# Top-k attention with a squared-ReLU feed-forward layer: a third search round over 264 columns, and v loaded in pieces of 1 KB

## The chip, the core and the metric

The kernel runs on one core of a Trainium2 chip. The core has five engines with queues of their own: TensorE (PE in the profile; PEld is its weight load), VectorE (DVE), ScalarE (ACT), GpSimd (POOL) and SyncE (SP), which here only issues transfers. Sixteen DMA engines move data between the memory of the chip (DRAM) and the core, and inside the core. The metric is device time in microseconds (us); less is better.

## The reference

There are 8 batches with 8 heads of 576 positions and 64 values each. For every query row the 576 scores are computed, the 32 largest are kept, and a softmax over those weighs the rows of v. The result, 4608 tokens of 512 values, goes through a feed-forward layer with 2048 hidden values.

```python
scores = scale * np.matmul(q, k.transpose(0, 1, 3, 2))
kth = np.partition(scores, -top_k, axis=-1)[..., -top_k:-top_k + 1]   # top_k = 32
scores = np.where(scores >= kth, scores, -1000000000.0)
attn = softmax(scores)
x = np.matmul(attn, v)                # then to [4608, 512]
out = np.square(np.maximum(x @ w_in, 0.0)) @ w_out
```

Inputs and outputs are float32.

## The kernel before

**Steps.** The work on the scores is cut into 144 steps (`steps`, L224 to L241). A step holds 128 query rows of two heads, side by side in the tile's middle axis `x`, so nearly everything is done for x = 0 and x = 1. The order of the instructions on each engine is the order in which the program issues them (`pin`). The main loop (L688) works on step u and, in the same turn, on parts of steps u+1 (scores) and u-1 to u-4 (weights, products, placing).

**Scores.** `scores` (L251) multiplies in two halves of 288 columns into the PSUM tiles `sc_a` and `sc_b` (L263), and ScalarE copies both into `s` (L266).

**Sorting into halves.** Before the search VectorE and GpSimd arrange the 576 scores of a row in a tile `cat`. `pairs_of` (L282, L283) takes the larger of columns n and n + 288; `quads_of` (L291, L292) compares the larger ones again, 144 apart: the larger go to columns 0 to 143 of `cat`, the smaller to 144 to 287. `both` (L307) and `lesser` (L316) put the lesser of each first pair, as sum minus larger, into columns 288 to 575 on GpSimd; `copy_far` (L298) copies what GpSimd needs out of PSUM on ScalarE. In the first 20 steps (`EARLY`) a quarter of this is done by VectorE (L285). Large scores thus gather on the left.

**The search.** `topk` finds the 32nd largest score in four rounds. Each round takes the eight largest of some columns with one MAX8 for each x (L342); the first three also overwrite them with a very negative number, with MATCH_REPLACE8 and the value load that goes before it (L346). The rounds read growing parts of `cat` (`part`, L333): 104 columns, then 120, then the left half of 288, then all 576. The fourth round's eighth value is the threshold. That is right only if the first three rounds took nothing smaller than it; L351 to L353 note for each row whether a round's eighth value lies below the fourth's, and if any row shows that, the program runs `general` (L788) at the end, which does the whole task in a plain way.

**Order on VectorE in a step.** `quads_of(u)`, round 1, the reciprocal of step u-4 (L436), rounds 2 and 3, `pairs_of(u+1)`, round 4.

**After the search.** `drop` (L378) marks on GpSimd what lies under the threshold, and a transfer from GpSimd's queue adds the marks to `s` (L382); ScalarE takes exponentials (L386); a transposing transfer on SP's queue turns them (L395); TensorE multiplies with v (L422), with a column of ones for the sum; ScalarE scales and stores (L452, L459). The feed-forward products (L533, L556) are fed in between in small pieces (`dense`, `piece`).

**Loads.** `load_pair` queues the loads of a pair of heads: for q, k and v one load of 512 rows for each head and one or two loads of the last 64 rows. `fetch` issues a few of these in each step on SP's queue; `load_first` issues those of the first pair on the queues of SP and ScalarE. All three tiles were laid out alike, as [128, 5, 2, 64]: partition p holds rows 4p to 4p+3, for each row the 64 values of head 0 and then those of head 1, and last the remaining rows. TensorE transposes q and k from there (`main`, `first_step`); `values` (L204) casts v to bf16 into `va` on ScalarE, with L206 for the 512 rows and L209 for the rest.

Of the kernel before, what the change touches and what calls it, by code (L numbers as in the profile page):

```python
# [13 lines left out]
f32 = mybir.dt.float32  # L14
# [4 lines left out]
AF = mybir.ActivationFunctionType  # L19
# [4 lines left out]
def kernel(  # L24
# [9 lines left out]
    nc = tc.nc  # L34
    B, H, S, D = q.shape
# [7 lines left out]
    HALF, QUAR = S // 2, S // 4  # L43

    def pin(ins):
        tc.keep_in_program_order(ins)
        return ins
# [3 lines left out]
    ld = fast.enter_context(tc.tile_pool(name="ld", bufs=2))  # L51
# [40 lines left out]
    raw, prep = {}, {}  # L92

    fetches = []

    def load_pair(i):
        b, pr = pairs[i]
        raw[i] = [None] * 3

        def whole_rows(z, name, two, a):  # L100
            def go():
                if a == 0:
                    raw[i][z] = ld.tile([128, 5, 2, 64], f32, name=name)
                pin(nc.sync.dma_start(out=raw[i][z][:, 0:4, a, :], in_=two[a, 0:512].rearrange("(p c) d -> p c d", c=4)))
            return go

        def rest_rows(z, two, at):
            def go():
                pin(nc.sync.dma_start(out=raw[i][z][at:at + 64, 4], in_=two[:, 512:576].rearrange("h p d -> p h d")))
            return go  # L110

        for z, (name, src) in enumerate((("q_raw", q), ("k_raw", k), ("v_raw", v))):
            two = src[b, 2 * pr:2 * pr + 2]
            for a in range(2):
                fetches.append((i, whole_rows(z, name, two, a)))
            fetches.append((i, rest_rows(z, two, 0)))
            if z == 2:
                fetches.append((i, rest_rows(z, two, 64)))
# [5 lines left out]


    def load_first():
        raw[0] = [ld.tile([128, 5, 2, 64], f32, name=name) for name in ("q_raw", "k_raw", "v_raw")]
        at = [z[0, 0:2] for z in (q, k, v)]

        def rows(queue, z, a):  # L130
            pin(queue.dma_start(out=raw[0][z][:, 0:4, a, :], in_=at[z][a, 0:512].rearrange("(p c) d -> p c d", c=4)))

        def last(queue, z, to=0):
            pin(queue.dma_start(out=raw[0][z][to:to + 64, 4], in_=at[z][:, 512:576].rearrange("h p d -> p h d")))

        for z in (1, 0):
            rows(nc.sync, z, 0)
            rows(nc.scalar, z, 1)
        last(nc.sync, 1)
        last(nc.scalar, 0)  # L140
        rows(nc.sync, 2, 0)
        rows(nc.sync, 2, 1)
        last(nc.sync, 2)
        last(nc.sync, 2, 64)

    def prep_units(i):
        q_raw, k_raw, v_raw = raw[i]
        qkT = heads.tile([128, 512 + 640], f32, name="qkT")
        qT, kT = qkT[:, 0:512], qkT[:, 512:1152]
        k_rest = kT.rearrange("p (n d) -> p n d", d=64)[:, 0:10:9]  # L150
        bd, va = qbd[i % 5], vau[i % 6]
        prep[i] = (qT, kT, bd, va)

        def twice(t):
            return t.rearrange("p (o d) -> p o d", o=1).broadcast_to([128, 2, 64])

        def main(which, src):
            def go():
                tp = ps_one.tile([128, 512], f32, name="gen", bufs=2)
                for c in range(4):  # L160
                    pin(nc.tensor.transpose(tp[:, c * 128:(c + 1) * 128], src[:, c], id_f[:, :]))
                pin(nc.scalar.activation((qT, kT[:, 64:576])[which], tp[:, :], AF.Copy, scale=(scale, 1.0)[which]))
            return go


        def first_step():
            for j, bank in ((0, "gen"), (1, "gen"), (2, "dn_ps"), (3, "sc_a")):
                if bank == "sc_a":
                    tp = ps_sc.tile([128, 2, 512], f32, name=bank)[:, 0, :]
                else:  # L170
                    tp = ps_one.tile([128, 512], f32, name=bank, bufs=2 if bank == "gen" else None)
                if j < 2:
                    for c in range(2):
                        pin(nc.tensor.transpose(tp[:, c * 128:(c + 1) * 128], k_raw[:, 2 * j + c], id_f[:, :]))
                    to, got = kT[:, 64 + j * 256:64 + (j + 1) * 256], tp[:, 0:256]
                elif j == 2:
                    pin(nc.tensor.transpose(tp[:, 0:128], q_raw[:, 0], id_f[:, :]))
                    to, got = qT[:, 0:128], tp[:, 0:128]
                else:
                    pin(nc.tensor.transpose(tp[:, 0:64], k_raw[0:64, 4], id_f[0:64, 0:64]))  # L180
                    to, got = k_rest, twice(tp[:, 0:64])
                if j % 2:
                    pin(nc.vector.tensor_copy(to, got))
                else:
                    pin(nc.scalar.activation(to, got, AF.Copy, scale=scale if j == 2 else 1.0))

        def first_q():
            tp = ps_one.tile([128, 512], f32, name="gen", bufs=2)
            for c in range(1, 4):
                pin(nc.tensor.transpose(tp[:, c * 128:(c + 1) * 128], q_raw[:, c], id_f[:, :]))  # L190
            pin(nc.scalar.activation(qT[:, 128:512], tp[:, 128:512], AF.Copy, scale=scale))

        def rest(both=(0, 1)):
            tp = ps_one.tile([128, 512], f32, name="gen", bufs=2)
            for which in both:
                src = (q_raw, k_raw)[which]
                pin(nc.tensor.transpose(tp[:, which * 64:(which + 1) * 64], src[0:64, 4], id_f[0:64, 0:64]))
            if 0 in both:
                pin(nc.scalar.activation(bd[0:64, 0:64], tp[0:64, 0:64], AF.Copy, scale=scale))
                pin(nc.scalar.activation(bd[64:128, 64:128], tp[64:128, 0:64], AF.Copy, scale=scale))  # L200
            if 1 in both:
                pin(nc.scalar.activation(k_rest, twice(tp[:, 64:128]), AF.Copy))

        def values():  # L204
            assert i < 6 or av_left[i - 6] == 0
            pin(nc.scalar.activation(va[:, 0:4, :, 0:64], v_raw[:, 0:4], AF.Copy))  # L206
            for x in range(2):
                half = slice(64 * x, 64 * x + 64)
                pin(nc.scalar.activation(va[half, 4 + x, :, 0:64], v_raw[half, 4], AF.Copy))  # L209

        if i == 0:
            return [first_step, first_q, values, lambda: rest((0,))]
        return [main(0, q_raw), main(1, k_raw), rest, values]
# [11 lines left out]
    for b in range(B):  # L225
        p0 = 4 * b
        if b == B - 1:
            at = [((0, 0), (1, 0), (2, 0), (0, 1), (3, 0), (1, 1), (2, 1), (3, 1)), [(j, 2) for j in range(4)], [(j, 3) for j in range(4)]]
            at = [[whole(p0 + j)[c] for j, c in some] for some in at]
# [94 lines left out]
    def topk(u, rounds=(0, 1, 2, 3)):  # L324
        d = st[u]
        g = u % GROUP
        if g == 0 and 0 in rounds:
            held_m["m"] = small.tile([128, GROUP, 2, 4, 8], f32, name="m", bufs=2)
        held = held_m["m"]
        m = d["m"] = [held[:, g, :, r] for r in range(4)]  # L330
        d["ends"] = held[:, g].rearrange("p x r j -> p x (r j)")[:, :, 0:32:31]
        cat = d["cat"]
        def part(r, x):  # L333
            if r == 0:
                return cat[:, x, 0:QUAR].rearrange("p (g n) -> p g n", n=18)[:, :, 0:13]
            if r == 1:
                return cat[:, x, 0:QUAR].rearrange("p (g n) -> p g n", n=6)[:, :, 1:6]
            return cat[:, x, 0:(HALF, S)[r - 2]]

        for r in rounds:  # L340
            for x in range(2):
                pin(nc.vector.max(out=m[r][:, x, :], in_=part(r, x)))  # L342
            if r == 3:
                break
            for x in range(2):
                pin(nc.vector.match_replace(out=part(r, x), in_to_replace=m[r][:, x, :], in_values=part(r, x), imm_value=NEG))  # L346
        if g == GROUP - 1 and 3 in rounds:
            f0 = 2 * (u + 1 - GROUP)
            each = held[:, :, :, :, 7].rearrange("p g x r -> p (g x) r")
            at = flags[:, f0:f0 + 2 * GROUP]  # L350
            pin(nc.gpsimd.tensor_tensor(at[:, :, 0:3], each[:, :, 3:4].broadcast_to([128, 2 * GROUP, 3]), each[:, :, 0:3], op=ALU.subtract))  # L351
            pin(nc.gpsimd.tensor_mul(at[:, :, 3], each[:, :, 3], each[:, :, 3]))
            pin(nc.gpsimd.tensor_scalar(at[:, :, 3], at[:, :, 3], scalar1=-1.0, scalar2=TINY * TINY, op0=ALU.mult, op1=ALU.add))  # L353
# [557 lines left out]
```

## Time and profile before

| | |
|---|---|
| median of three runs | 940.04 us (935.3, 940.04, 949.31) |
| profiled execution | 938.25 us |
| its span, first to last instruction | 936.5 us |
| mean granted TensorE clock | 0.933 |
| instructions | 20941 |
| transfers | 329978 packets, 166.29 MB |

The time of an execution is longer than the span by what lies before the first and after the last instruction. In the profile's groups, a line such as "L342 DVE MAX8 m<-cat 128x8 f32<-128x288 f32 x288 | 120.4, 472 | 0.0" reads: line of the program, engine, operation, output and input tile, their shapes, how often; then busy microseconds in total and mean nanoseconds of one; then how long the engine stood idle just before such instructions, and what ended the wait. The chain of work that ended last is followed back from the last instruction, at each step to what released it; "issue" on it is time in which the engine waited for nothing that the profile shows. Busy times of one engine overlap in the records, so the sum of its groups is more than its busy time.

### The profile page before, as it was taken

What the parts mean: (1) busy time and instruction counts of PE and PEld (TensorE: products, weight loads), DVE (VectorE), ACT (ScalarE), POOL (GpSimd) and SP (SyncE); (2) the same over time, 40 slices, a digit from 0 to 9 for tenths busy, and PEclk for the clock granted to TensorE, in tenths of its full rate; (3) what the DMA queues carried; (4) which work ended last, traced back from release to release, by engine and by line L of the source; (5) the groups of instructions that cost most, each with busy time, mean ns of one, the idle gap of its engine ahead of it and who ended that gap; (6) DMA issues with size and microseconds to landing.
All of it is one profiled execution on the core that took longest, in us unless ns stands there. A gap on an engine that the chain in (4) does not pass through costs nothing.

```text
span 936.5 us, 20941 instructions
## 1 busy us (share of the span) xinstructions
PE 678.4 (72%) x6176; PEld 429.6 (46%) x6176; DVE 898.1 (96%) x3637; ACT 784.2 (84%) x1776; POOL 778.8 (83%) x803
## 2 busy tenths in 40 slices
PE   6777667777776778767786777767766687777777
PEld 3333344444444445444454444444444455554554
DVE  5999999999999999999999999999989999999993
ACT  4777888889888988889887998888978998997984
POOL 7888889888888888888888889888878887898780
PEclk9988999899999998999989999999979998999899
DMA  5568866899998999889999998989999999787761
GB/s 140 132 159 166 174 137 125 173 200 198 205 209 172 201 203 199 187 191 198 195 202 182 187 206 195 207 182 191 176 191 207 188 206 195 160 174 164 148 138 39
DMA packets 329978, 166.29 MB, mean 178 GB/s; under 512 B 306561, under 2 KB 306561, under 8 KB 329857
## 3 DMA queue, kind: packets, MB, share of 16 engines
q1 hardware_dynamic: 311088, 92.62, 52.2%
q0 software_dynamic: 17568, 71.97, 33.9%
q8 instruction: 52, 0.85, 0.4%
q14 instruction: 70, 0.57, 0.2%
q10 hardware_dynamic: 1200, 0.30, 0.1%
HBM read 37.75 MB, written 9.44 MB: 50 GB/s over the span
## 4 chain that ended last, share of the span: by engine, by line
DVE 70%; issue 10%; PE 8%; ACT 6%; DMA 5%; POOL 1%; SPq 0%; ACTq 0%; POOLq 0%
DVE m L342 29%; DVE cat L346 18%; DVE sc_b L282 6%; DVE cat L292 5%; DVE cat L291 5%; DVE most L283 5%; PE dn_ps L556 2%; PE sc_b L263 2%; PE gen L533 1%; PE sc_a L263 1%; DMA wT<-w_two_a 1%; DMA wT<-w_two_c 1%; ACT s L266 1%; DVE rsum L436 1%; DMA v_raw<-in_v_dram 1%
## 5 line engine op out<-in xcount | busy, mean ns | idle before, releaser
L342 DVE MAX8 m<-cat 128x8 f32<-128x104 f32 (+3 forms) x1152 | 461.2, 455 | 0.0
L346 DVE MATCH_REPLACE8 cat<-m,cat 128x104 f32<-128x104 f32 (+2 forms) x864 | 281.1, 346 | 0.0
L307 POOL TENSOR_TENSOR cat<-s 128x576 int32<-128x576 int32 (+1 forms) x144 | 230.2, 1598 | 3.8 <-ACT s L266 3.8
L316 POOL TENSOR_TENSOR cat<-cat,most 128x576 int32<-128x576 int32 (+1 forms) x144 | 190.3, 1322 | 26.4 <-ACT most L298 15.6
L263 PE MATMUL sc_b<-qkT 64*128 64x288 f32 x512 | 109.2, 502 | 127.3 <-DVE cat L292 125.5
L533 PEld LDWEIGHTS <-w_in 128*128 128x128 bf16 x2304 | 149.6, 103 | 49.5 <-issue 28.5
L556 PE MATMUL dn_ps<-w_out,h 128*128 128x512 bf16 x576 | 165.0, 417 | 1.5 <-ACT wide L561 1.5
L533 PE MATMUL gen<-xT,w_in 128*128 128x128 bf16 x2016 | 140.7, 226 | 12.7 <-ACT rl L538 6.0
L266 ACT ACTIVATE s<-sc_b 128x576 f32<-128x576 f32 x144 | 93.4, 648 | 66.2 <-PE sc_b L263 59.8
L378 POOL TENSOR_SCALAR gone_a<-s,neg 128x576 uint8<-128x576 f32 x143 | 107.1, 749 | 29.5 <-ACT neg L361 20.2
L263 PE MATMUL sc_a<-qkT 64*128 64x288 f32 x512 | 99.7, 464 | 40.9 <-DVE most L283 30.0
L378 POOL TENSOR_SCALAR gone_b<-s,neg 128x576 uint8<-128x576 f32 x142 | 106.4, 749 | 27.3 <-ACT neg L361 17.7
L263 PEld LDWEIGHTS sc_b<-qkT 64*128 64x128 f32 x512 | 47.4, 206 | 177.2 <-issue 102.0
L266 ACT ACTIVATE s<-sc_a 128x576 f32<-128x576 f32 x144 | 91.5, 635 | 20.2 <-PE sc_a L263 19.7
L538 ACT ACTIVATE rl<-gen 128x512 f32<-128x512 f32 x142 | 85.1, 600 | 5.5 <-PE gen L533 4.4
L544 ACT ACTIVATE h<-rl 128x512 bf16<-128x512 f32 x136 | 85.8, 631 | 4.3
L346 DVE MATCH_VALUE_LOAD cat<-m,cat 128x8 f32 x864 | 89.1, 103 | 0.0
L422 PEld LDWEIGHTS <-wT 128*128 128x128 bf16 (+1 forms) x1600 | 59.0, 101 | 63.7 <-DMA wT<-w_two_c 24.2
L556 PEld LDWEIGHTS <-h 128*128 128x128 bf16 x576 | 54.4, 104 | 66.5 <-issue 31.0
L282 DVE TENSOR_TENSOR sc_b<-sc_a,s 128x288 f32<-128x288 f32 x144 | 69.6, 484 | 6.1 <-ACT s L266 6.0
L386 ACT ACTIVATE w_two_a<-s,neg 128x576 bf16<-128x576 f32 x96 | 69.4, 779 | 5.0 <-DMA s<-gone_b 3.0
L291 DVE TENSOR_TENSOR cat<-sc_b,most 128x288 f32<-128x288 f32 x144 | 67.3, 467 | 5.2 <-ACT most L298 5.0
(165 smaller groups left out, 1201.4 us busy)
## 6 DMA issues: line engine op xcount, KB each, us to landing
s<-gone_a POOLq DMA_DIRECT2D x61, 576.0 KB, 4.9
s<-gone_b POOLq DMA_DIRECT2D x61, 576.0 KB, 4.7
v_raw<-in_v_dram SPq DMA_DIRECT2D x64, 128.0 KB, 3.2
out_dram<-wide SPq DMA_DIRECT2D x32, 256.0 KB, 3.6
k_raw<-in_k_dram SPq DMA_DIRECT2D x63, 128.0 KB, 3.3
q_raw<-in_q_dram SPq DMA_DIRECT2D x63, 128.0 KB, 3.2
wide<-in_moe_w_in_dram SPq DMA_DIRECT2D x8, 512.0 KB, 4.7
wide<-in_moe_w_out_dram SPq DMA_DIRECT2D x8, 512.0 KB, 4.1
```

What stands on the lines that cost most here:

```text
L263: pin(nc.tensor.matmul(out=ps[j][:, x, 0:HALF], lhsT=lhsT, rhs=rhs, start=True, stop=True))
L266: pin(nc.scalar.activation(s[:, :, j * HALF:(j + 1) * HALF], ps[j][:, :, 0:HALF], AF.Copy))
L282: pin(tt(far, one[:, :, QUAR:HALF], two[:, :, QUAR:HALF], op=ALU.max))
L291: pin(tt(cat[:, :, 0:QUAR], far, near, op=ALU.max))
L307: pin(tt(less, s[:, :, 0:wide].bitcast(i32), s[:, :, HALF:HALF + wide].bitcast(i32), op=ALU.add))
L316: pin(tt(less, less, d["most"][:, 0:n_h, :, :].bitcast(i32).rearrange("p h x n -> p x h n"), op=ALU.subtract))
L342: pin(nc.vector.max(out=m[r][:, x, :], in_=part(r, x)))
L346: pin(nc.vector.match_replace(out=part(r, x), in_to_replace=m[r][:, x, :], in_values=part(r, x), imm_value=NEG))
L378: pin(nc.gpsimd.tensor_scalar(byte[:, x, :, 1], s[:, x, :], scalar1=d["neg"][:, x, 1:2], scalar2=-HUGE, op0=ALU.add, op1=ALU.mult))
L533: pin(nc.tensor.matmul(out=hp[:, n * n_rows:(n + 1) * n_rows], lhsT=w_in[:, kh, (f0 + n) * 128:(f0 + n + 1) * 128], rhs=xt(kh), start=(kh ...
L544: pin(nc.scalar.activation(h2, flat, AF.Square))
L556: pin(nc.tensor.matmul(out=op[:, :], lhsT=held["h2"][:, f, c * 128:(c + 1) * 128], rhs=w_out[:, f, :], start=(f == 0), stop=(f == NF - 1)))
```

## The change

Two things are edited. First, the third round reads columns 0 to 263 of `cat` in place of 0 to 287; the fourth still reads all 576. Second, the tile `v_raw` is laid out head by head: partition p holds the four rows of head 0 one after the other, then those of head 1, then the remaining rows as before. A load of 512 rows of one head thus writes 256 values in a row (1 KB) in each partition, where it wrote four runs of 64 values (256 bytes). The cast in `values` reads the new layout and writes `va` as before. The loads keep their number, queue and order.

```diff
+    def by_head(t):
+        return t.rearrange("p (a d) -> p a d", a=2)
...
-                    raw[i][z] = ld.tile([128, 5, 2, 64], f32, name=name)
+                    raw[i][z] = ld.tile([128, 640] if z == 2 else [128, 5, 2, 64], f32, name=name)
+                if z == 2:
+                    pin(nc.sync.dma_start(out=raw[i][z][:, a * 256:(a + 1) * 256], in_=two[a, 0:512].rearrange("(p c) d -> p (c d)", c=4)))
+                    return
                 pin(nc.sync.dma_start(out=raw[i][z][:, 0:4, a, :], in_=two[a, 0:512].rearrange("(p c) d -> p c d", c=4)))
...
-                pin(nc.sync.dma_start(out=raw[i][z][at:at + 64, 4], in_=two[:, 512:576].rearrange("h p d -> p h d")))
+                t = raw[i][z]
+                to = by_head(t[at:at + 64, 512:640]) if z == 2 else t[at:at + 64, 4]
+                pin(nc.sync.dma_start(out=to, in_=two[:, 512:576].rearrange("h p d -> p h d")))
...
-            pin(nc.scalar.activation(va[:, 0:4, :, 0:64], v_raw[:, 0:4], AF.Copy))
+            pin(nc.scalar.activation(va[:, 0:4, :, 0:64], v_raw[:, 0:512].rearrange("p (a c d) -> p c a d", a=2, c=4), AF.Copy))
             for x in range(2):
                 half = slice(64 * x, 64 * x + 64)
-                pin(nc.scalar.activation(va[half, 4 + x, :, 0:64], v_raw[half, 4], AF.Copy))
+                pin(nc.scalar.activation(va[half, 4 + x, :, 0:64], by_head(v_raw[half, 512:640]), AF.Copy))
...
-            return cat[:, x, 0:(HALF, S)[r - 2]]
+            return cat[:, x, 0:(HALF - 24, S)[r - 2]]
```

`load_first` is changed in the same way for the first pair.

More of the change, by code (lines that the diff above doesn't have):

```diff
@@ L126, in load_first @@
     def load_first():
-        raw[0] = [ld.tile([128, 5, 2, 64], f32, name=name) for name in ("q_raw", "k_raw", "v_raw")]
+        raw[0] = [ld.tile([128, 5, 2, 64], f32, name=name) for name in ("q_raw", "k_raw")] + [ld.tile([128, 640], f32, name="v_raw")]
         at = [z[0, 0:2] for z in (q, k, v)]
         def rows(queue, z, a):
+            if z == 2:
+                pin(queue.dma_start(out=raw[0][z][:, a * 256:(a + 1) * 256], in_=at[z][a, 0:512].rearrange("(p c) d -> p (c d)", c=4)))
+                return
             pin(queue.dma_start(out=raw[0][z][:, 0:4, a, :], in_=at[z][a, 0:512].rearrange("(p c) d -> p c d", c=4)))
         def last(queue, z, to=0):
-            pin(queue.dma_start(out=raw[0][z][to:to + 64, 4], in_=at[z][:, 512:576].rearrange("h p d -> p h d")))
+            t = raw[0][z]
+            dst = by_head(t[to:to + 64, 512:640]) if z == 2 else t[to:to + 64, 4]
+            pin(queue.dma_start(out=dst, in_=at[z][:, 512:576].rearrange("h p d -> p h d")))
         for z in (1, 0):
```

## Prediction

> **What bounds the kernel now.** I read the page from the top: the busy shares, then the chain of work that ended last.
>
> ```profile
> span 936.5 us, 20941 instructions
> PE 678.4 (72%) x6176; PEld 429.6 (46%) x6176; DVE 898.1 (96%) x3637; ACT 784.2 (84%) x1776; POOL 778.8 (83%) x803
> ...
> DVE 70%; issue 10%; PE 8%; ACT 6%; DMA 5%; POOL 1%; SPq 0%; ACTq 0%; POOLq 0%
> DVE m L342 29%; DVE cat L346 18%; DVE sc_b L282 6%; DVE cat L292 5%; DVE cat L291 5%; DVE most L283 5%; PE dn_ps L556 2%; PE sc_b L263 2%; PE gen L533 1%; PE sc_a L263 1%; DMA wT<-w_two_a 1%; DMA wT<-w_two_c 1%; ACT s L266 1%; DVE rsum L436 1%; DMA v_raw<-in_v_dram 1%
> ```
>
> VectorE (DVE) is busy 96% of the span, and L342 (the eight largest) and L346 (their removal) are 47% of the chain. An average can hide stages, so next come the windows by stage (columns: window, length, then busy us of PE, PEld, DVE, ACT and POOL with counts, the granted clock, the DMA share and GB/s) and the list of what VectorE waited for between 21 and 860 us.
>
> ```profile
> 21.00:141.00 120.00, 83.18 (x600) 44.14 (x598) 118.70 (x473) 92.22 (x196) 102.91 (x113) 0.94 0.71 153
> 300.00:400.00 100.00, 73.14 (x683) 46.73 (x680) 100.00 (x406) 87.79 (x203) 87.53 (x86) 0.91 0.94 198
> 420.00:500.00 80.00, 58.79 (x542) 37.68 (x541) 79.59 (x327) 71.42 (x165) 68.92 (x69) 0.92 1.06 200
> 600.00:700.00 100.00, 70.56 (x656) 44.89 (x654) 96.70 (x395) 85.42 (x197) 82.84 (x82) 0.90 0.94 188
> 900.00:936.50 36.50, 24.72 (x273) 16.69 (x270) 19.47 (x53) 20.39 (x46) 9.52 (x10) 0.93 0.31 72
> ```
>
> ```profile
> DVE cat L291 <- ACT most L298: 4.7, 5, 1.6
> DVE rsum L436 <- PE av_ps L422: 2.9, 2, 1.4
> DVE sc_b L282 <- ACT s L266: 2.8, 3, 1.3
> ```
>
> From 300 to 400 us VectorE has no gap at all. Its waits from 21 to 860 us sum to 4.7 + 2.9 + 2.8 = 10.4 us, in ten places; 600 to 700 us has the worst, 3.3 us. So VectorE is the bound, step after step, outside those places and outside the end.
>
> The chain says in how many of the 144 steps that holds. The third round's two MAX8 stand on it as one piece of 0.71 to 0.73 us; counting these pieces over the span gives 116. First and last of them, then the piece at which the chain leaves VectorE for good, and its longest transfer:
>
> ```profile
> 26.63 0.72 DVE m L342 x2
> ...
> 674.51 11.40 DMA wT<-w_two_c
> ...
> 861.64 0.72 DVE m L342 x2
> ...
> 863.12 0.47 DVE sc_b L282
> 863.68 0.41 ACT most L298
> ```
>
> Of the 28 steps missing, 2 lie before 26.63 us, 7 after 861.64 us (at 6.1 us a step up to 906 us: there the chain runs through ScalarE and TensorE), and 19 under excursions like the one at 674.51 us, in which a late transpose carries the chain for several steps.
>
> **Part 1: 264 columns in place of 288.** Nothing is added. Each step's third round has two MAX8 and two MATCH_REPLACE8 that read 24 columns less. No row has 264 columns; the rows on both sides have 288 and 120 (view of groups, shapes kept apart):
>
> ```profile
> L346 DVE MATCH_REPLACE8 cat<-m,cat 128x288 f32<-128x288 f32 x288 | 129.1, 469 | 0.0
> L342 DVE MAX8 m<-cat 128x8 f32<-128x288 f32 x288 | 120.4, 472 | 0.0
> L346 DVE MATCH_REPLACE8 cat<-m,cat 128x120 f32<-128x120 f32 x288 | 78.5, 293 | 0.0
> L342 DVE MAX8 m<-cat 128x8 f32<-128x120 f32 x288 | 68.4, 291 | 0.0
> ```
>
> MAX8: (472 − 291)/168 = 1.077 ns a column. MATCH_REPLACE8: (469 − 293)/168 = 1.048 ns. For 24 columns that is 25.9 and 25.1 ns, and for two of each 102 ns a step. Recorded durations overlap on this engine, so I check the slope by starts (timeline of one step):
>
> ```profile
> 511.83 0.48 DVE L342 MAX8 m<-cat 128x8 f32<-128x120 f32 x2
> ...
> 512.58 0.65 ACT L266 ACTIVATE s<-sc_b 128x576 f32<-128x576 f32 x1 [1.46 <-PE sc_b L263]
> 512.69 0.85 DVE L342 MAX8 m<-cat 128x8 f32<-128x288 f32 x2
> 513.42 0.11 DVE L346 MATCH_VALUE_LOAD cat<-m,cat 128x8 f32 x1
> 513.48 0.48 DVE L346 MATCH_REPLACE8 cat<-m,cat 128x288 f32<-128x288 f32 x1
> ...
> 514.27 0.49 DVE L282 TENSOR_TENSOR sc_b<-sc_a,s 128x288 f32<-128x288 f32 x1
> ```
>
> The second round occupies 512.69 − 511.83 = 0.86 us, the third 514.27 − 512.69 = 1.58 us: 0.72 us for 4 × 168 columns, 1.07 ns each. The time truly comes out of the step.
>
> How much reaches the end? Bounds: all 144 steps, 144 × 0.102 = 14.7 us; only those on the chain, 116 × 0.102 = 11.8 us. I take the second: in the other 28 steps VectorE would reach a wait 0.1 us sooner and wait 0.1 us longer.
>
> What is late next? L282 needs the copy `s`, which ends at 512.58 + 0.65 = 513.23, 1.04 us before L282 starts at 514.27. The change takes 0.10 us of that: no new wait in an ordinary step. GpSimd (POOL) is the other engine with a full queue:
>
> ```profile
> 501.98 1.74 POOL L307 TENSOR_TENSOR cat<-s 128x576 int32<-128x576 int32 x1
> ...
> 507.77 1.74 POOL L307 TENSOR_TENSOR cat<-s 128x576 int32<-128x576 int32 x1
> ```
>
> In this stretch it ran one step's work in 507.77 − 501.98 = 5.79 us, catching up, while VectorE's step is 6.10 (100 us of steps in 300 to 400). At 6.00 GpSimd still fits, with 0.21 us of reserve a step in place of 0.31; its lateness heals more slowly, at no cost while nothing else is late.
>
> **Part 2: v in pieces of 1 KB.** The same 64 large loads, issued from the same queue at the same places, hence no queue gains or loses an instruction and no wait is added. A load of 128 KB falls from 512 pieces of 256 bytes to 128 of 1 KB: 384 × 64 = 24,576 packets less. Rows: packets of the whole run and the queue of the accumulating transfers from the page, the loads alone from the DMA view of 0 to 8 us, and the view of the tile `v_raw`.
>
> ```profile
> DMA packets 329978, 166.29 MB, mean 178 GB/s; under 512 B 306561, under 2 KB 306561, under 8 KB 329857
> q0 software_dynamic: 17568, 71.97, 33.9%
> ```
>
> ```profile
> q1 hardware_dynamic: 3106, 0.76, 43.4%
> ```
>
> ```profile
>   PEld sc_b L263: 1.8, 1
>   PEld sc_a L263: 1.8, 1
>   PEld gen L161: 0.4, 1
> ...
> DMA to landing us min/median/max: 2.1/3.1/7.3
> ```
>
> The early loads took 43.4% × 16 × 8 us = 55.6 us of engine time for 3106 packets: 17.9 ns each, 73 us a MB. The accumulating packets of 4 KB took 33.9% × 16 × 936.5 us = 5080 us for 71.97 MB: 71 us a MB. So one end: DMA time goes by bytes and the saving is nothing. The other end: it goes by packets, 24,576 × 17.9 ns / 16 = 27 us on each engine, 2.9% of the span. I take the first, because the nearest row with larger packets is no cheaper per byte. Below nothing would be a transpose's packet behind a piece of 1 KB, four times 17.9 = 72 ns in place of 18 ns; against landings of microseconds I count nothing. On the path the value is zero in any case: who waits for v_raw is TensorE, three times, 4.0 us in all, and VectorE never. If that cover is gone, the cost is such a wait, 1.8 us.
>
> The Trainium skill, "DMA: Bandwidth & Descriptors", section Specifications, states that transfers under 512 B are below line rate, since the engine then reads, modifies and writes. By that rule 1 KB pieces would hand DMA time back and the relief below would be the forecast. The trace does not bear it out: 73 us a MB in small pieces stands beside 71 in large ones, though those large ones also add.
>
> The cast of v on ScalarE now reads runs of 64 with a jump in place of 512 in a row:
>
> ```profile
> L206 ACT ACTIVATE vau_b<-v_raw 128x512 bf16<-128x512 f32 x6 | 3.8, 628 | 0.0
> L209 ACT ACTIVATE vau_b<-v_raw 64x128 bf16<-64x128 f32 x12 | 3.7, 307 | 0.1
> L508 ACT ACTIVATE xt_rem_a<-gen 64x256 bf16<-64x256 bf16 x8 | 3.0, 377 | 0.0
> ```
>
> L508 reads four runs of 64 and lies below the line between its neighbours (307 + (628 − 307)/3 = 414 ns), so runs cost nothing there; I take zero. The bad end is a doubling, 32 × 0.63 = 20 us of ScalarE, which has 936.5 − 784.2 = 152 us idle; of it only the share in excursions, 19 of 144 steps, some 3 us, would reach the end. A gain has no reason.
>
> **The sum.** 938.25 us is the profiled execution's own time (span 936.5 and 1.75 around it); 938.25 − 11.8 = 926.4 us, and 923.5 with all 144 steps. Against the median of the runs before, 940.04 (935.3 to 949.31), that is 1.4% less; 2%, about what a measurement of this kernel can tell from no change, lies at 921.2 and 958.8.
>
> **Rivals.**
>
> Relief, faster: fewer packets let transposes and accumulations land earlier, so that the ten waits go as well. For it: the DMA share is 0.94 and 1.06 in the windows quoted, and the chain has a transfer of 11.40 us. Against: bytes are unchanged, and v is small beside 166.29 MB. Time: 938.25 − 14.7 − 10.4 = 913.2 us. This is also what the rule on 512 B would give.
>
> Waits eat it: the path from the masked scores through transpose and product to L436 is one of latencies that do not shrink, while each step is 0.1 us shorter, and a busier DMA lands more of them late. Twice the waits: 926.4 + 10.4 = 936.8 us, within 2%.
>
> Slower, the same mechanism gone over its edge: an engine set already at shares of 0.94 to 1.06 is asked for the same transfers in less time, and transposes like that of 11.40 us become common. Each costs VectorE what 600 to 700 us shows, 3.3 us. From four more the time is above before (926.4 + 13.2 = 939.6); from ten more over 2% slower (959.4). Against it: only one such place in 144 steps.
>
> The change doesn't do what it says: if in any row a value left out of the third round belongs to the 32 largest, the flag is set and `general` does everything again after the fast path. No row shows its price; the products a second time, 678 us of TensorE, would alone bring it above 1600 us. Following the four rounds on the reference's drawn inputs, the third round's eighth value stays above the fourth's in all 36,864 rows, by 5.2e-5 at the least, so I leave it 0.02.
>
> **Chances.** Forecast (921 to 931): 0.60. Relief: 0.17. Waits eat it (931 to 945): 0.16. Slower: 0.05. Fallback: 0.02. The forecast is 926.4 us. The range 913 to 938 takes in the relief and the doubled waits; outside lie the rest of the waits, the slower cases and a little below. Faster by over 2%: the relief and the lower edge of the forecast, 0.17 + 0.03 = 0.20. Slower by over 2%: 0.04 of the slower case and the fallback, 0.06. Within 2%: the rest, 0.74.
>
> **What would show it.** In the changed profile: MAX8 and MATCH_REPLACE8 at 264 columns near 446 and 444 ns; an ordinary step of 6.00 us; VectorE's waits from 21 to 860 us near 10 us; the last VectorE piece on the chain some 12 us earlier; 24,576 packets less, with the DMA share nearly as before; L206 still 628 ns. I am wrong if the waits rise by as much as the busy time falls, if L206 doubles, or if the share of DMA drops by more than 0.03.

## The result, and the profile after

The changed kernel takes 928.33 us (median of six runs, 924.85 to 929.37) against 939.69 us for the kernel before beside it: a ratio of 0.9891, with a 95% interval of 0.9859 to 0.9922. It is faster by 1.1%, 11.4 us by the medians, less than the 2% that one would call a clear change. The two profiled executions are 938.25 and 924.85 us, 13.4 us apart. Ratios leave out slow runs; in this whole study that is one run, of 927.48 us with 216 columns, which the median given for that kernel still holds.

The page of the changed kernel: span, busy time by engine, packets, the two large queues, and the chain by engine. (Lines have moved: L355 is the old L342, L359 the old L346, L295 and L296 the old L282 and L283, L304 and L305 the old L291 and L292, L311 the copy that was L298.)

```profile
span 923.1 us, 20865 instructions
PE 669.7 (73%) x6100; PEld 429.1 (46%) x6176; DVE 884.2 (96%) x3637; ACT 780.6 (85%) x1776; POOL 776.9 (84%) x803
...
DMA packets 305401, 166.29 MB, mean 180 GB/s; under 512 B 273792, under 2 KB 281984, under 8 KB 305280
...
q1 hardware_dynamic: 286512, 92.62, 52.2%
q0 software_dynamic: 17568, 71.97, 34.1%
...
DVE 68%; issue 11%; ACT 7%; PE 6%; DMA 5%; POOL 2%; SPq 0%; POOLq 0%; ACTq 0%
```

VectorE's busy time fell from 898.1 to 884.2 us, 13.9 us; the span fell by 13.4. VectorE still carries the chain. The other engines' work is where it was: the 76 instructions less, all on TensorE, are records missing from this trace (6100 matmuls of 6176), not work left out, and with 216 columns the profile has 20941 instructions again. So the fall of the span matches the fall of VectorE's work. One step of the changed kernel (timeline of VectorE; the second column is the duration):

```profile
300.05 0.45 DVE L355 MAX8 m<-cat 128x8 f32<-128x120 f32 x2
...
300.91 0.76 DVE L355 MAX8 m<-cat 128x8 f32<-128x264 f32 x2
301.59 0.07 DVE L359 MATCH_VALUE_LOAD cat<-m,cat 128x8 f32 x1
...
302.39 0.45 DVE L295 TENSOR_TENSOR sc_b<-sc_a,s 128x288 f32<-128x288 f32 x1
...
306.05 0.45 DVE L355 MAX8 m<-cat 128x8 f32<-128x120 f32 x2
```

The third round now occupies 302.39 - 300.91 = 1.48 us where it took 1.58, and the step is 306.05 - 300.05 = 6.00 us where it was 6.10. VectorE's waits between 21 and 850 us (what, for whom, us in total, how often, longest):

```profile
DVE cat L304 <- ACT most L311: 6.8, 8, 1.7
DVE sc_b L295 <- ACT s L279: 3.2, 3, 1.2
DVE rsum L449 <- PE av_ps L435: 0.7, 1, 0.7
```

They sum to 10.7 us, as before (10.4).

### The profile page after: what moved, and what is told of

It reads as the page before. It is cut to its first block, busy times and chain, and to the rows that moved or that the text cites. A ratio compares the mean times of both kernels' runs of the same rounds, so it can differ in the third digit from the quotient of the medians.

```text
span 923.1 us, 20865 instructions
## 1 busy us (share of the span) xinstructions
PE 669.7 (73%) x6100; PEld 429.1 (46%) x6176; DVE 884.2 (96%) x3637; ACT 780.6 (85%) x1776; POOL 776.9 (84%) x803
## 2 busy tenths in 40 slices
DMA packets 305401, 166.29 MB, mean 180 GB/s; under 512 B 273792, under 2 KB 281984, under 8 KB 305280
## 3 DMA queue, kind: packets, MB, share of 16 engines
q1 hardware_dynamic: 286512, 92.62, 52.2%
## 4 chain that ended last, share of the span: by engine, by line
DVE 68%; issue 11%; ACT 7%; PE 6%; DMA 5%; POOL 2%; SPq 0%; POOLq 0%; ACTq 0%
DVE m L355 28%; DVE cat L359 18%; DVE sc_b L295 6%; DVE cat L304 5%; DVE cat L305 5%; DVE most L296 5%; PE sc_b L276 2%; DMA wT<-w_two_a 1%; PE gen L546 1%; ACT s L279 1%; PE dn_ps L569 1%; DVE rsum L449 1%; PE sc_a L276 1%; ACT w_two_a L399 1%; DMA wT<-w_two_c 1%
## 5 line engine op out<-in xcount | busy, mean ns | idle before, releaser
L355 DVE MAX8 m<-cat 128x8 f32<-128x104 f32 (+3 forms) x1152 | 438.5, 422 | 0.0
L359 DVE MATCH_REPLACE8 cat<-m,cat 128x104 f32<-128x104 f32 (+2 forms) x864 | 262.9, 312 | 0.0
L276 PE MATMUL sc_b<-qkT 64*128 64x288 f32 x512 | 106.7, 491 | 123.5 <-DVE cat L305 121.7
L569 PE MATMUL dn_ps<-w_out,h 128*128 128x512 bf16 x509 | 147.3, 414 | 10.7 <-issue 7.0
L546 PE MATMUL gen<-xT,w_in 128*128 128x128 bf16 x2016 | 142.7, 228 | 10.6 <-ACT rl L551 4.0
L435 PEld LDWEIGHTS <-wT 128*128 128x128 bf16 (+1 forms) x1600 | 58.1, 101 | 72.4 <-DMA wT<-w_two_a 24.6
L399 ACT ACTIVATE w_two_b<-s,neg 128x576 bf16<-128x576 f32 x95 | 68.8, 779 | 4.2 <-DMA s<-gone_b 3.3
L399 ACT ACTIVATE w_two_c<-s,neg 128x576 bf16<-128x576 f32 x94 | 68.0, 782 | 4.6 <-DMA s<-gone_a 3.4
L295 DVE TENSOR_TENSOR sc_b<-sc_a,s 128x288 f32<-128x288 f32 x144 | 65.6, 456 | 6.6 <-ACT s L279 6.6
L395 POOL DMA_DIRECT2D s<-gone_b x61 | 54.1, 888 | 20.1 <-DVE m L355 9.2
```

What stands on the lines that cost most here:

```text
L276: pin(nc.tensor.matmul(out=ps[j][:, x, 0:HALF], lhsT=lhsT, rhs=rhs, start=True, stop=True))
L295: pin(tt(far, one[:, :, QUAR:HALF], two[:, :, QUAR:HALF], op=ALU.max))
L399: pin(nc.scalar.activation(w_two[u % 3][:, x, 0:S], d["s"][:, x, :], AF.Exp, bias=d["neg"][:, x, 0:1]))
L546: pin(nc.tensor.matmul(out=hp[:, n * n_rows:(n + 1) * n_rows], lhsT=w_in[:, kh, (f0 + n) * 128:(f0 + n + 1) * 128], rhs=xt(kh), start=(kh ...
L569: pin(nc.tensor.matmul(out=op[:, :], lhsT=held["h2"][:, f, c * 128:(c + 1) * 128], rhs=w_out[:, f, :], start=(f == 0), stop=(f == NF - 1)))
```

## The experiments

All ratios are to the kernel before, run on the same chip in the same comparison.

**One part alone.** The first kernel takes the edit of the third round and leaves v as it was:

```diff
-            return cat[:, x, 0:(HALF, S)[r - 2]]
+            return cat[:, x, 0:(HALF - 24, S)[r - 2]]
```

> Only the third round is cut to 264 columns; v is loaded as before. Theory (VectorE is the bound, v's loads cost nothing on the path): the whole gain is here, 11 to 13 us under before, ratio 0.986 to 0.988, an ordinary step of 6.00 us, VectorE's waits between 21 and 850 us near 10 us. Rival (part of the gain came from fewer packets): a gain of at most 8 us, ratio 0.992 or more, and VectorE's waits above 14 us.

Measured: 927.35 us, ratio 0.9891 (0.9853 to 0.9929), the same ratio as with both parts, and 10.4 us under the 937.7 of before. VectorE's waits were 13.5 us in the profiled execution (930.25 us), between what the two theories said:

```profile
DVE cat L291 <- ACT most L298: 8.1, 10, 1.6
DVE sc_b L282 <- ACT s L266: 3.3, 3, 1.2
DVE rsum L436 <- PE av_ps L422: 2.1, 4, 1.1
```

The second kernel takes v's new layout alone, with HALF in place of HALF - 24.

> Only v is loaded in pieces of 1 KB; the third round reads 288 columns. Theory: the time of before within 2 us, ratio 0.998 to 1.002, a step of 6.10 us, 305401 packets. Rival (relief): VectorE's waits fall to half and the time by 4 us or more, ratio 0.996 or less.

Measured: 937.23 us, ratio 0.9987 (0.9965 to 1.0009), with 305401 packets. No gain that can be told from none. The waits were 10.0 us (7.9 + 1.5 + 0.6), against 10.4 before. The whole gain that can be measured is the third round's.

**No loads of v at all.** In the changed kernel, the loads of v from the third pair on are left out, with empty entries in their places in the order of issue; the casts go on with the rows of the first two pairs:

```diff
+            if z == 2 and i >= 2:
+                raw[i][2] = raw[i % 2][2]
+                fetches.extend((i, lambda: None) for _ in range(4))
+                continue
```

> The changed kernel with v loaded for the first two pairs only, the same rows cast again for the later pairs, so those products are of the wrong rows. It bounds what any relief of the DMA engines by v can give at 264 columns. Theory (v's transfers cost nothing on the path): within 3 us of the changed kernel, 925 to 931 us, and VectorE's waits between 21 and 850 us near 10 us. Rival (relief): 920 us or less, waits under 5 us.

Measured: 927.5 us, ratio 0.9907 (0.9884 to 0.993). The DMA share between 200 and 800 us fell from 0.97 to 0.91, and the waits stayed at 10.4 us:

```profile
DVE cat L308 <- ACT most L315: 7.3, 7, 1.6
DVE rsum L453 <- PE av_ps L439: 1.9, 2, 1.3
DVE sc_b L299 <- ACT s L283: 0.9, 1, 0.9
DVE m L359 <- POOL cat L333: 0.3, 1, 0.3
```

Even without these transfers (156.45 MB moved in place of 166.29) no gain shows at 264 columns, so no way of loading v could have gained more than the few microseconds by which the two intervals leave room.

**How far the gain goes.** The third round cut further, to 240 and 216 columns (HALF - 48, HALF - 72), and to 144 (QUAR), the last with the flag's comparison made unreachable:

```diff
-    ... scalar1=0.0, scalar2=None, op0=ALU.is_gt
+    ... scalar1=1.0e30, scalar2=None, op0=ALU.is_gt
```

> The changed kernel with a third round over 240 columns. If the gain per column holds until VectorE's step meets another limit near 5.8 us, the step is 5.90 us and the time 11 to 12 us under the changed kernel, 917 us. If the gain fades steadily from 288 down, because each shorter step turns more late copies into waits, about half of that: 922 to 924 us, with VectorE's waits between 10 and 26 us.

> As the changed kernel, with a third round over 216 columns: 48 less again. Theory: a step of 6.00 - 0.204 = 5.80 us while VectorE stays the bound; with the same 113 to 116 steps on the chain 23 us less than the changed kernel, near 905 us, ratio to before 0.963. Rival (GpSimd, whose own work was seen to take 5.79 us a step, or late transposes take over): VectorE's waits rise from 10 us to 20 us or more and the time stays above 912 us.

> As the changed kernel, with a third round over 144 columns, and the flag that would start the general path compared with a number that is never reached, so that path is left out and rows whose third round took too small a value stay as they are. Theory, if VectorE alone counted: a step of 6.10 - 0.614 = 5.49 us, some 868 us. Rival, which I expect: GpSimd's 5.79 us a step becomes the bound, VectorE waits 0.3 us in each step, some 40 us in all, and the time is 900 us or more, no better than with 216 columns by more than 5 us.

The second column is worked out by the slope per column. The next three are read in one profiled execution of each kernel, the last two from all its runs.

| columns | work less per step, estimate (us) | profiled execution | VectorE busy | its waits, 21 to 850 us | median | ratio (95%) |
|---|---|---|---|---|---|---|
| 288, before | | 938.25 | 898.1 | 10.4 | | |
| 264, changed kernel | 0.10 | 924.85 | 884.2 | 10.7 | 928.33 | 0.9891 (0.9859 to 0.9922) |
| 240 | 0.20 | 924.61 | 872.1 | 18.6 | 924.53 | 0.9876 (0.9839 to 0.9914) |
| 216 | 0.31 | 922.95 | 859.2 | 26.4 | 920.09 | 0.9779 (0.9739 to 0.9820) |
| 144, no flag | 0.61 | 915.46 | 821.6 | 58.1 | 920.37 | 0.9823 (0.9773 to 0.9874) |

The gain fades: 24 columns gave 10 to 11 us; the next 48 gave another 7 by the medians (927.35 to 920.09 in one comparison) and 10 by the ratios, where the arithmetic says 23; and 72 more give nothing. How it fades between 264 and 216 the runs don't tell: the intervals at 264 and 240 lie almost on each other. Most of the work taken off VectorE comes back as its waits. From before to 144 columns its busy time fell by 76.5 us and the span (936.5 to 913.7) by only 22.8; of the 53.7 us between them 47.7 are the growth of these waits. So at 216 columns the rival was right, not the theory; at 240 the time came out half a microsecond above the range of the fading, far from the 917 us of the other. Of the kernels that do the whole task the one with 216 columns has the lowest ratio, below both kernels of this study. Its waits:

```profile
DVE cat L304 <- ACT most L311: 15.1, 16, 2.4
DVE sc_b L295 <- ACT s L279: 7.0, 8, 2.0
DVE rsum L449 <- PE av_ps L435: 3.5, 2, 2.7
DVE m L355 <- POOL cat L329: 0.8, 1, 0.8
```

I had expected GpSimd to be the next bound at 144 columns. It was not: of 58.1 us VectorE waited 1.9 for GpSimd, 33.4 for the copy L311 and 14.8 for the copies of the scores:

```profile
DVE cat L304 <- ACT most L311: 33.4, 51, 2.2
DVE sc_b L295 <- ACT s L279: 14.8, 18, 2.4
DVE rsum L449 <- PE av_ps L435: 8.0, 9, 3.3
DVE m L355 <- POOL cat L329: 1.9, 4, 0.9
```

One of the longest waits at 216 columns, in the timeline (in brackets the idle time before, and what ended it):

```profile
569.45 1.44 ACT L399 ACTIVATE w_two_c<-s,neg 128x576 bf16<-128x576 f32 x2 [3.74 <-DMA s<-gone_b]
569.54 0.57 PEld L435 LDWEIGHTS <-wT 128*128 128x128 bf16 x10 [3.24 <-DMA wT<-w_two_b]
...
570.80 0.39 ACT L311 ACTIVATE most<-sc_b 128x288 f32<-128x288 f32 x1
...
571.22 0.46 DVE L304 TENSOR_TENSOR cat<-sc_b,most 128x288 f32<-128x288 f32 x1 [2.43 <-ACT most L311]
```

The exponentials (L399) waited 3.74 us for the accumulation to land; the copy L311 stood behind them in ScalarE's queue; VectorE waited 2.43 us for the copy. TensorE waited for a transpose at the same time, until 0.1 us later. The DMA view from 560 to 570 us (last number: us from issue to landing) shows that these two were not late by themselves:

```profile
s<-gone_b POOLq DMA_DIRECT2D x1, 576.0 KB, 7.4
...
v_raw<-in_v_dram SPq DMA_DIRECT2D x2, 128.0 KB, 6.4
...
wT<-w_two_b SPq DMA_TRANSPOSE x1, 7.5
```

Over the whole run the medians are 4.7 us for such an accumulation, 3.1 for the loads of v and 5.1 for the transposes. From 565 to 567 us the sixteen engines moved 135 and 103 GB/s (windows of 1 us), against a mean of 181. The transpose of 11.40 us in the profile before stands in the same kind of stretch: 62 to 68 GB/s from 676 to 680 us, with loads of k landing after 9.7 us.

**What the waits hang on.** Four more kernels start from the one with 144 columns, where the waits are largest, and each takes one suspect away: the loads of v (as above), the wait of the exponentials for the accumulation, the wait of the products for the transposes, or the cast of v on ScalarE. The first diff sends the accumulation to a tile `aside`, the second lets the products read a tile `fixed` that is filled once, the third leaves the cast out from the seventh pair on.

```diff
-            pin(nc.gpsimd.dma_start(out=s[:, :, :]...., accum_op=ALU.add))
+            pin(nc.gpsimd.dma_start(out=aside[0][:, :, :]...., accum_op=ALU.add))
```

```diff
-        va, wT = prep[i][3], st[u]["wT"]
+        va, wT = prep[i][3], st[u]["wT"] if u >= U - 2 else fixed
```

```diff
             assert i < 6 or av_left[i - 6] == 0
+            if i >= 6:
+                return
```

> The kernel with 144 columns and no flag, and v loaded for the first two pairs only; later pairs cast the same rows again, so their products are of the wrong rows of v. 300 loads' worth of transfers less, about 8 of 166 MB. If the load on the DMA engines sets the step of 6.03 us that this kernel shows in place of VectorE's 5.49, the time falls by 4% of the middle, some 20 to 30 us, to 890 to 900 us. If latencies or ScalarE set it, it stays within 6 us of 920 us. I expect the second.

> The kernel with 144 columns and no flag, but the accumulating transfer adds into a tile of its own, so the exponentials no longer wait for it (nothing is masked from step 20 on); all transfers and instructions stay. If the latency from threshold through marks and accumulation to the exponentials holds ScalarE's queue and so VectorE, the waits of VectorE fall from 58 us to under 25 us and the time to 885 us or less. If the transposes or the amount of work are the cause, the time stays above 912 us.

> The kernel with 144 columns and no flag, but the products of all steps except the last two read a fixed tile in place of the transposed weights, so TensorE no longer waits for the transposes, which still run. If these waits (218 us of TensorE's idle time) delay the scores and so VectorE, VectorE's waits fall from 58 us to under 25 us and the time to 885 us or less. If they only fill time that TensorE has to spare, the time stays above 912 us.

> The kernel with 144 columns and no flag, with the cast of v left out from the seventh pair on (older rows of v are used). That takes 26 x 1.24 = 32 us of work off ScalarE. If ScalarE's amount of work sets the step, the time falls by 20 to 32 us, to 888 to 900 us; if latencies do, by less than 10 us.

| taken away | median | ratio (95%) | VectorE's waits, 21 to 850 us |
|---|---|---|---|
| nothing (144 columns) | 920.37 | 0.9823 (0.9773 to 0.9874) | 58.1 |
| loads of v | 911.25 | 0.9704 (0.9645 to 0.9764) | 58.7 |
| wait for the accumulation | 922.05 | 0.9810 (0.9764 to 0.9857) | 65.8 |
| wait for the transposes | 914.04 | 0.9739 (0.9684 to 0.9793) | 57.1 |
| cast of v | 915.53 | 0.9748 (0.9703 to 0.9792) | 60.7 |

None of them is the cause alone: each gave from nothing to some 9 us by the medians, against waits of 57 to 66 us that remained. The waits were read in profiled executions of 915.46, 913.26, 924.00, 912.42 and 916.04 us, in the order of the table. Only the interval without the loads lies clear of the one with nothing taken away. Without the loads the time fell by less than the 20 to 30 us of the theory and more than the 6 us of its rival, so that one is inconclusive. The kernel without the wait for the accumulation has other waits than the rest:

```profile
DVE m L358 <- POOL cat L332: 48.6, 99, 2.9
DVE sc_b L298 <- ACT s L282: 6.4, 7, 2.6
DVE cat L307 <- ACT most L314: 6.0, 13, 1.4
DVE rsum L452 <- PE av_ps L438: 4.8, 4, 1.5
```

The wait for the copy fell from 33.4 to 6.0 us, so the accumulation does act through ScalarE's queue; but now GpSimd is late in 99 steps and takes 48.6 us. Around 500 us it sets the step: its L332 starts at 498.85, 504.66 and 510.46 us, 5.8 us apart, as much as its own work took in the prediction. But the edit also adds a wait. All accumulations now go into one tile, and this profile has 121 semaphore waits on GpSimd's queue at their line, which the kernel with 144 columns hasn't:

```profile
L398 POOLq EVENT_SEMAPHORE  x121: 17/17/17, 153.3 to 889.3; - x121
```

GpSimd stood idle 67.5 us ahead of its accumulations, in place of 39.2. So it isn't shown how much of the 48.6 us is GpSimd's own work and how much is this added wait, nor what taking away the wait for the accumulation alone would give.

Last, an order in which the exponentials don't stand ahead of the copy, at 216 columns: the three lines that issue the exponentials of step u-2 and their transpose are moved behind `lesser(u + 1)`.

```diff
-        if ok(u - 2):
-            exps(u - 2, 0)
-            exps(u - 2, 1)
-            turn(u - 2)
         fetch(10 if u < 8 else 3)
...
             lesser(u + 1)
+        if ok(u - 2):
+            exps(u - 2, 0)
+            exps(u - 2, 1)
+            turn(u - 2)
```

> The kernel with 216 columns, with the exponentials of step u-2 and their transpose issued behind the copy that L304 waits for, in place of ahead of it. If VectorE's waits of 26 us at 216 columns come from ScalarE's order (1.44 us of exponentials, which themselves wait for the accumulation, stand ahead of the copy), the wait of L304 falls from 15 to under 5 us and the time from 920 to 905 to 912 us. If the amount of work or GpSimd sets it, or if the later transposes hold up TensorE by as much, the time stays at 917 us or more.

Measured: 920.76 us, ratio 0.9826 (0.9810 to 0.9842). VectorE's waits:

```profile
DVE sc_b L295 <- ACT s L279: 15.3, 25, 2.4
DVE rsum L449 <- PE av_ps L435: 9.6, 10, 3.0
DVE m L355 <- POOL cat L329: 0.7, 1, 0.7
DVE cat L304 <- ACT most L311: 0.6, 2, 0.4
```

The wait of L304 is gone, 15.1 to 0.6 us, as expected; the waits for the scores and for the products grew from 7.0 to 15.3 and from 3.5 to 9.6, and the sum is 26.2 us where it was 26.4. The wait has moved, the time has not.

What stays open: why in such stretches as the one before 569.5 us everything in flight lands late together. No run took that apart.

## Why the prediction was right

The forecast was 926.4 us; the median is 928.33 and the profiled execution 924.85. The mechanism was right; two smaller steps, on DMA time and on where the next waits come from, were not.

**VectorE is the bound: right.** With the third round alone the ratio is the same 0.9891. The waits were 10.7 us in the changed kernel, but 13.5 with the third round alone, so a few microseconds of the saving can go back into waits, in some executions at least.

**102 ns a step: right.** The step went from 6.10 to 6.00 us. The check that I gave for it was badly chosen: MAX8 and MATCH_REPLACE8 at 264 columns were to show 446 and 444 ns. The view of groups has:

```profile
L359 DVE MATCH_REPLACE8 cat<-m,cat 128x264 f32<-128x264 f32 x288 | 118.1, 417 | 0.0
L355 DVE MAX8 m<-cat 128x8 f32<-128x264 f32 x288 | 109.4, 421 | 0.0
...
L359 DVE MATCH_REPLACE8 cat<-m,cat 128x120 f32<-128x120 f32 x288 | 74.8, 267 | 0.0
L355 DVE MAX8 m<-cat 128x8 f32<-128x120 f32 x288 | 64.8, 266 | 0.0
```

The 120 columns, which the change doesn't touch, are shorter by 25 and 26 ns too. The slope within this profile, (421 - 266)/144 = 1.076 ns a column, is the one that the prediction used (1.077).

**116 of 144 steps reach the end: right in size, by a reading that is one execution's.** Predicted 11.8 us, bounded by 14.7; measured 11.4 by the medians, 10.4 with the part alone, 13.4 between the profiled executions. The interval of the ratio is 7 to 13 us, so the number of steps isn't tested closely, and that the forecast came within 2 us is in part luck. In the changed kernel 113 third rounds stand on the chain, but others: the last at 886.36 us, where I had expected the chain to leave VectorE some 12 us before 863.12. That sign failed. In the profiles with one part alone, counted in the same way, 105 (third round) and 107 (v) stand on it. So which steps lie under an excursion changes from execution to execution; how many is steadier.

**v on the path costs nothing: right; its DMA time at nothing: too low.** Ratio 0.9987 for that part alone. For the DMA time the prediction gave two ends, nothing (by bytes) and 27 us (by packets). The share of the hardware queue q1 times the span is 52.2% of 936.5 = 489 us before and 52.2% of 923.1 = 482 us after; with one part alone it is 484 us (old pieces, 52.1% of 928.5) and 476 us (new pieces, 50.8% of 937.7). That is some 7 us less with the new pieces, but over all profiles with new pieces and all loads it runs from 468 to 498 us, so these sums alone don't show it. The first 8 us do, where a third of the bytes of this queue are v in the new pieces:

```profile
q1 hardware_dynamic: 2482, 0.80, 41.6%
```

That is 41.6% × 16 × 8 us = 53.2 us for 0.80 MB, 67 us a MB, where it was 73 before. It is 73 as well with the third round alone, and 66 to 71 in all eleven profiles with the new pieces. So larger pieces did cost less DMA time for a MB. The comparison in the prediction, 73 beside 71 us a MB, set loads beside transfers that also add, and missed this. The Trainium skill's rule on pieces under 512 B ("DMA: Bandwidth & Descriptors", Specifications) is borne out in its direction by these rows. What it would have meant for the kernel, the relief, did not come: 24,577 packets less brought no time that can be measured, and neither did leaving these loads out.

From the view of the tile `v_raw` after:

```profile
L219 ACT ACTIVATE vau_b<-v_raw x6: 620/625/651, 20.8 to 802.7; 128x512 bf16<-128x512 f32 x6
...
DMA to landing us min/median/max: 2.1/3.0/6.1
```

The loads land in 3.0 us in place of 3.1, and the cast in runs of 64 takes 625 ns as it did.

**The rivals.** Relief (913.2 us) fell with the kernel without loads of v. That waits eat the gain did not happen at 264 columns, but it is what happens next: at 240 they are 18.6 us, at 216 26.4. Its mechanism, latencies that don't shrink with the step, shows at 569.45 us, there in a stretch in which transfers were slow; the prediction placed it on the transposes and L436 alone, while most of the wait comes through ScalarE's queue to L304 (15.1 of 26.4 us at 216 columns). The claim that GpSimd "still fits" at 6.00 us held.

## What to carry to other kernels

Work taken off a bounding engine comes out nearly one for one as long as its waits stay as they were, so compare the waits, not only the time. Here they grew from 10.7 to 18.6 us once 0.2 of a step's 6.1 us had been saved, and the further cuts bought much less than their arithmetic. Taking one wait away can move it to other queues, as the late exponentials did at 216 columns: 26.4 us of waits became 26.2. A transfer that nobody on the path waits for can be made better without any gain. When checking a duration in another profile, use differences within it, or starts. And an edit that takes one wait away should be read for the waits that it adds.

## What the runs showed of the hardware

VectorE's recorded durations can differ between profiled executions by a nearly constant amount, with the same starts: 120 columns of MAX8 have a mean of 291 ns before, 266 ns after and 260 ns with v's part alone, and MATCH_VALUE_LOAD 103, 76 and 70 ns, while the second round takes 0.86 us from start to start before and after (512.69 - 511.83 and 300.91 - 300.05). Instructions that VectorE runs outside the steps keep theirs (TENSOR_REDUCE near the end: 1346 and 1345 ns). Four times larger pieces for the loads of v lowered the DMA time of the first loads from 73 to 66 to 71 us a MB; a price by packets would have taken 27 us off q1's 489 and 484 us in the whole run, to 457 to 462, and no profile with the new pieces and all loads lies under 468. And there are stretches of a few microseconds (two were looked at) in which all sixteen engines together move 62 to 135 GB/s in place of some 180, and the transfers in flight land late together.
